# Decoding float64 weights with one shift: bytes landed one off, the sign made by ScalarE

## The chip, the cores and the metric

The kernel runs on one core of one Trainium2 chip. The metric is the device time of one launch in microseconds (us). The kernel before was timed three times: median 725.14 us, lowest 724.97, highest 725.63.

TensorE (PE) multiplies and transposes, VectorE (DVE), ScalarE (ACT) and GpSimd (POOL) do the elementwise work, SyncE (SP) issues the DMAs. Each engine works through its own list of instructions in order.

## The reference

Attention with a window of 128 keys and 4 sink keys, for 4 batches, 8 heads, 768 positions and 64 dimensions a head, and behind it a feed-forward block over the 3072 rows of 512 numbers that the heads make together:

```python
scores = np.where(keep, scale * q @ k.T, -1e9)      # keep: sink or in window
a = np.exp(scores - max); a = a / (sum + 1e-9)
x = (a @ v) -> [3072, 512]
h = x @ w_in                                         # [512, 2048]
g = np.where(h >= 1, h, np.where(h <= -1, 0, (h + 1) ** 2 / 4))
out = g @ w_out                                      # [2048, 512]
```

The weights `w_in` and `w_out` are float64 and are handed to the kernel as 8-byte words; q, k and v are float32.

## The kernel before, in words

**Units and chunks.** A unit is one head of one batch at one half of the positions: three tiles of 128 queries. Eight units (the heads) make a chunk of 384 rows, and there are eight chunks. The attention of chunk c+1 runs beside the feed-forward block of chunk c, so at the start there is only attention, and beside it the decoding of weights.

**One unit** goes through `scores` (three products into PSUM; DVE finds the row maxima while it evacuates, line 253; ACT takes the exponential, line 257; POOL and DVE make the reciprocals of the sums, lines 262 and 263; then three instructions scale the three tiles, lines 273 to 277), `transp` (two groups of TensorE transposes, copied out by ACT, lines 329 and 333) and, for the first 16 units ("native"), `av2`, which multiplies two units at once with their values (line 369; ACT copies the result, line 371, and `split` makes its coarse part, line 475). `NORM` says for a native unit which engine scales which tile: `"vaa"` is DVE for the first and ACT for the other two.

**Weights.** They come as 32 blocks of 128 x 512 float64: 16 of `w_in` and 16 of `w_out` in turn. `weights(n)` fetches block n and up to three after it into raw tiles (512 KB each) and calls `decode`: from the two 32-bit halves of each float64, three DVE instructions (lines 157 to 159) make the bits of a float32; ACT rounds it to the matrix type (line 160) and DVE subtracts to get the remainder (line 161). So a block costs four DVE instructions and one of ACT. `WFIRST = 13` blocks are spread over the attention of the first chunk, the other 19 over the feed-forward block of the first chunk.

**Feed-forward block.** `stage1` makes h for 128 of the 2048 columns and g from it (lines 452 to 455), split into gh and gl (line 456: on POOL in the first chunk, by `GL_POOL`, on DVE in the others); `stage2` multiplies with `w_o`.

**What sets the order.** TensorE's order is that of the program, as `spread` mixes the lists of steps. For the other engines a planner orders the instructions at build time; `issue_after` keeps a decode behind the row maximum issued last. The DMAs of the start stay in program order on SP (`keep_in_program_order`): the values of a pair (`v_s`, two buffers) wait for the product of the pair two before, and the weight blocks behind them in SP's list wait too.

**Rounds.** Between 13 and 54 us TensorE goes through the same round four times: scores of a unit, transposes of the unit before, scores of the next unit, transposes of the first, values product of a finished pair (`av2`). The rounds below are numbered 1 to 4; round 1 takes the scores of units 2 and 3, round 4 those of 8 and 9. From 54 us on the feed-forward block runs beside the attention.

## Time and profile before

| | |
|---|---|
| median of three runs | 725.14 us |
| profiled execution | 726.5 us |
| its span, first to last instruction | 724.8 us |
| mean granted TensorE clock | 0.992 of 2.4 GHz |
| PE, DVE, ACT, POOL busy | 699.7, 529.4, 504.4, 305.7 us |

The profiled execution took 726.5 us, 1.7 us more than its span and 1.4 us more than the median of the timed runs. "Busy" is the time in which an engine has an instruction in work; instructions of DVE and ACT overlap the next one by about 0.1 us, so that a queue that never waits advances by the distance of the starts, not by the durations.

### The profile page before, as it was taken

What the parts mean: (1) busy time and instruction counts of PE and PEld (TensorE: products, weight loads), DVE (VectorE), ACT (ScalarE), POOL (GpSimd) and SP (SyncE); (2) the same over time, 40 slices, a digit from 0 to 9 for tenths busy, and PEclk for the clock granted to TensorE, in tenths of its full rate; (3) what the DMA queues carried; (4) which work ended last, traced back from release to release, by engine and by line L of the source; (5) the groups of instructions that cost most, each with busy time, mean ns of one, the idle gap of its engine ahead of it and who ended that gap; (6) DMA issues with size and microseconds to landing.
All of it is one profiled execution on the core that took longest, in us unless ns stands there. A gap on an engine that the chain in (4) does not pass through costs nothing.

```text
span 724.8 us, 12264 instructions
## 1 busy us (share of the span) xinstructions
PE 699.7 (97%) x3841; PEld 615.6 (85%) x3841; DVE 529.4 (73%) x1393; ACT 504.4 (70%) x1313; POOL 305.7 (42%) x529
## 2 busy tenths in 40 slices
PE   6879999999999999999999999999999999999996
PEld 4547778899989999999889998999989989989895
DVE  8988989578786777687887887878877787833221
ACT  5887677687776777687677877778777867644432
POOL 3002224755453545455564666645556365500000
PEclk9989999999999999999999999999999999999999
DMA  7453453222221322153242533334323342101001
GB/s 291 146 225 127 188 193 121 58 89 58 57 57 33 96 65 66 46 186 114 88 125 64 170 126 115 115 103 137 122 82 127 107 125 74 67 1 44 0 1 48
DMA packets 38568, 73.54 MB, mean 101 GB/s; under 512 B 6752, under 2 KB 21088, under 8 KB 38496
## 3 DMA queue, kind: packets, MB, share of 16 engines
q1 hardware_dynamic: 38496, 72.68, 31.2%
q8 instruction: 32, 0.52, 0.3%
q14 instruction: 40, 0.33, 0.1%
HBM read 66.37 MB, written 6.29 MB: 100 GB/s over the span
## 4 chain that ended last, share of the span: by engine, by line
PE 70%; DVE 13%; ACT 6%; DMA 5%; POOL 3%; issue 2%; POOLq 0%; ACTq 0%; SPq 0%; DVEq 0%
PE h_ps L445 28%; PE o_ps L464 28%; PE ps_a L249 6%; PE ps_a L404 4%; ACT p L257 2%; PE ps_a L336 2%; DVE k_s L233 2%; DMA k_r<-qk 1%; DVE p L277 1%; PE ps_a L369 1%; PE ps_a L326 1%; DMA r<-vx 1%; DVE gl L456 1%; ACT k_s L231 1%; DMA r<-qk 1%
## 5 line engine op out<-in xcount | busy, mean ns | idle before, releaser
L445 PE MATMUL h_ps<-x,wi 128*128 128x384 f32 x1536 | 310.1, 340 | 0.0
L445 PEld LDWEIGHTS h_ps<-x,wi 128*128 128x128 f32 x1536 | 262.7, 188 | 10.8 <-issue 2.7
L464 PE MATMUL o_ps<-w,gh 128*128 128x512 f32 x768 | 243.6, 398 | 0.0
L464 PE MATMUL o_ps<-w,gl 128*128 128x512 f32 x384 | 150.9, 393 | 0.3 <-POOL gl L456 0.3
L464 PEld LDWEIGHTS o_ps<-w,gh 128*128 128x128 f32 x768 | 134.1, 188 | 15.8 <-issue 1.4
L454 DVE SCALAR_TENSOR_TENSOR g<-g,h_ps 128x384 f32<-128x384 f32 x128 | 70.2, 548 | 66.4 <-ACT g L453 65.5
L452 ACT ACTIVATE g<-h_ps,half 128x384 f32<-128x384 f32 x128 | 73.9, 577 | 62.0 <-PE h_ps L445 61.6
L257 ACT ACTIVATE p<-p,peak 128x260 f32<-128x260 f32 (+1 forms) x192 | 94.0, 490 | 30.7 <-DVE peak L253 29.2
L235 POOL TENSOR_TENSOR q_l<-r,q_h 128x384 fp32r<-128x384 f32 x48 | 50.4, 1049 | 131.9 <-ACT q_h L234 121.6
L455 ACT CAST gh<-g 128x384 fp32r<-128x384 f32 x128 | 65.5, 511 | 53.0 <-DVE g L454 52.1
L456 DVE TENSOR_TENSOR gl<-g,gh 128x384 fp32r<-128x384 f32 x112 | 70.2, 627 | 24.7 <-ACT gh L455 23.7
L464 PEld LDWEIGHTS o_ps<-w,gl 128*128 128x128 f32 x384 | 72.0, 188 | 18.2 <-POOL gl L456 0.8
L253 DVE CUSTOM_DVE_ANT_0 p<-ps_a,m 128x260 f32<-128x260 f32 (+1 forms) x176 | 68.2, 398 | 16.6 <-PE ps_a L249 15.9
L233 DVE TENSOR_TENSOR k_s<-k_r,k_s 64x524 fp32r<-64x524 f32 (+1 forms) x44 | 47.2, 1073 | 42.8 <-ACT k_s L231 42.7
L453 ACT ACTIVATE g<-g 128x384 f32<-128x384 f32 x128 | 67.0, 524 | 2.6
L348 POOL TENSOR_SCALAR_AFFINE_SELECT pt<-pt 128x384 fp32r<-128x384 f32 (+1 forms) x96 | 50.3, 525 | 23.8 <-DVE pt L341 21.8
L277 DVE TENSOR_SCALAR p<-p,stat 128x132 f32<-128x132 f32 (+1 forms) x160 | 56.8, 404 | 0.2
L262 POOL TENSOR_SCALAR stat<-stat 128x3 f32<-128x3 f32 x64 | 28.6, 447 | 66.1 <-ACT p L257 61.4
L346 POOL TENSOR_SCALAR_AFFINE_SELECT pt<-pt 128x384 fp32r<-128x384 f32 (+1 forms) x96 | 52.6, 549 | 6.9 <-ACT pt L340 2.7
L404 PEld LDWEIGHTS ps_a<-pt,v_s 128*128 128x128 f32 x304 | 46.5, 188 | 2.2
L404 PE MATMUL ps_a<-pt,v_s 128*128 128x256 f32 (+1 forms) x304 | 46.4, 272 | 0.0
L249 PE MATMUL ps_a<-k_s,q_h 128*128 128x260 f32 (+1 forms) x144 | 40.4, 281 | 4.4 <-DVE sk L343 3.1
(116 smaller groups left out, 986.1 us busy)
## 6 DMA issues: line engine op xcount, KB each, us to landing
r<-qk SPq DMA_DIRECT2D x48, 192.0 KB
k_r<-qk SPq DMA_DIRECT2D x32, 262.0 KB
w<-w_in SPq DMA_DIRECT2D x16, 512.0 KB
w<-w_out SPq DMA_DIRECT2D x16, 512.0 KB
again<-w_in SPq DMA_DIRECT2D x16, 512.0 KB
again<-w_out SPq DMA_DIRECT2D x16, 512.0 KB
out<-o SPq DMA_DIRECT2D x23, 256.0 KB
r<-vx SPq DMA_DIRECT2D x32, 128.0 KB
```

Source lines behind the costliest of these rows:

```text
L249: nc.tensor.matmul(ps[:, lo:260], lhsT=q[:, i * P:(i + 1) * P], rhs=k_s[:, c0:c0 + 260 - lo], start=(j == 0), stop=(j == len(qs) - 1))
L253: found = nc.vector.tensor_tensor_reduce(out=p[:, i, lo:260], in0=ps[:, lo:260], in1=m, scale=-0.125, scalar=3.0e38, op0=ALU.add, op1=ALU. ...
L257: nc.scalar.activation(p[:, i, lo:260], p[:, i, lo:260], AF.Exp, bias=peak_i, scale=-1.0, accum_out=stat[:, i:i + 1])
L277: (nc.gpsimd if eng == "p" else nc.vector).tensor_scalar(p[:, i, lo:260], p[:, i, lo:260], r, None, op0=ALU.mult)
L404: nc.tensor.matmul(z, lhsT=w, rhs=y, start=(n == 0), stop=(n == len(mms) - 1))
L445: nc.tensor.matmul(h_ps[:, :T], lhsT=w_i[j][:, w, ct * P:(ct + 1) * P], rhs=x[:, y, ct], start=(ct == 0 and n == 0), stop=(ct == NCT - 1 a ...
L452: nc.scalar.activation(g, h_ps[:, :T], AF.Relu, bias=half, scale=0.5)
L453: nc.scalar.activation(g, g, AF.Square)
L454: nc.vector.scalar_tensor_tensor(g, g, 1.0, h_ps[:, :T], op0=ALU.min, op1=ALU.max)
L455: nc.scalar.copy(gh, g)
L456: (nc.gpsimd if row0 == GL_POOL else nc.vector).tensor_tensor(gl, g, gh.bitcast(F32), op=ALU.subtract)
L464: nc.tensor.matmul(o_ps[tt], lhsT=gg[:, tt * P:(tt + 1) * P], rhs=w_o[j][:, w], start=(j == 0 and n == 0), stop=(j == NJ - 1 and n == 2))
```

## The change

Four edits go together.

- A raw tile is 8 bytes a partition longer, and the block lands one byte further, from byte 1. The 32-bit word 1 of the tile then holds bytes 3 to 6 of the first float64, so that one shift right by 5 gives the lower 27 bits of the float32. The top byte (sign and upper exponent bits) lies at byte 8, the first of word 2.
- `quick` replaces `decode` for the planned blocks: ACT reads the top bytes as uint8, scales and adds so that the low bits of the float32 which it writes hold the wanted five bits (Relu with a scale and a per-partition bias, into word 2); DVE shifts word 1 in place; one DVE instruction shifts word 2 left by 27 and joins both; then rounding and subtraction as before (`parts`). A block now costs three DVE instructions and two of ACT.
- `NORM` is "vva": DVE scales two tiles of a native unit, ACT one. `GL_POOL` is gone: gl is always made by DVE.
- `WFIRST` is 10: ten blocks beside the first chunk's attention, 22 beside its feed-forward block.

```diff
-GL_POOL = 0
-NORM = "vaa"
+NORM = ("vva", "vva")
-WFIRST = 13
+WFIRST = 10
+STEP = 1.125 + 2.0 ** -12
+BASE = 2.0 ** 23 - 31.5
...
+    base = const.tile([P, 1], F32, name="base")
+    nc.gpsimd.memset(base, BASE)
...
+    def parts(t, w):
+        nc.scalar.copy(t[:, 0], w)
+        nc.vector.tensor_tensor(t[:, 1], w, t[:, 0].bitcast(F32), op=ALU.subtract)
...
+    def quick(t, w, words):
+        x, top = words[:, 1:-1:2], words[:, 2::2]
+        nc.scalar.activation(top.bitcast(F32), words.bitcast(U8)[:, 8::8], AF.Relu, bias=base, scale=STEP)
+        nc.vector.tensor_scalar(x, x, 5, None, op0=ALU.logical_shift_right)
+        nc.vector.scalar_tensor_tensor(w, top, 27, x, op0=ALU.logical_shift_left, op1=ALU.bitwise_or)
+        parts(t, w.bitcast(F32))
...
-                    raw[k] = wpool.tile([P, 2 * DM], I32, name="w")
-                    fetch(raw[k], (w_in, w_out)[k % 2][k // 2].bitcast(I32))
+                    raw[k] = wpool.tile([P, 2 * DM + 2], I32, name="w")
+                    fetch(raw[k].bitcast(U8)[:, 1:8 * DM + 1], (w_in, w_out)[k % 2][k // 2].bitcast(U8))
...
-                decode((w_i, w_o)[i][j], moe.tile([P, DM], I32, name="o"), words)
+                quick((w_i, w_o)[i][j], moe.tile([P, DM], I32, name="o"), raw[n])
...
-            eng = NORM[i] if units.index(u) < NATIVE else "v"
+            eng = NORM[units.index(u) // H][i] if units.index(u) < NATIVE else "v"
...
-        (nc.gpsimd if row0 == GL_POOL else nc.vector).tensor_tensor(gl, g, gh.bitcast(F32), op=ALU.subtract)
+        nc.vector.tensor_tensor(gl, g, gh.bitcast(F32), op=ALU.subtract)
```

The planner puts the lists of DVE and ACT in a new order. On ACT, round 2, from behind the copy of the values product to the scaling of unit 4 (line 275; p_366 is unit 4, p_407 unit 5), before:

```order
L160 CAST wi2_153<-o_358 128x512
L160 CAST w_318<-o_319 128x512
L475 CAST x_657<-xn_169 128x384
L257 ACTIVATE p_366,stat_367<-p_366,peak_97 128x128
L257 ACTIVATE p_366,stat_367<-p_366,peak_97 128x260
L329 COPY pt_335<-ps_a_394 128x2x128
L333 COPY spn3_146<-ps_a_394 4x128
L329 COPY pt_335<-ps_a_400 128x3x128
L257 ACTIVATE p_366,stat_367<-p_366,peak_97 128x260
L257 ACTIVATE p_407,stat_408<-p_407,peak_97 128x128
L257 ACTIVATE p_407,stat_408<-p_407,peak_97 128x260
L275 ACTIVATE p_366<-p_366,stat_367 128x260 x2
```

and now, where line 175 is the new Relu, 273 the exponential and 291 the scaling (w_349 is the first block that is fetched in this round, p_360 unit 4, p_400 unit 5):

```order
L159 CAST w_351<-o_352 128x512
L491 CAST x_634<-xn_171 128x384 [waits Activation_49]
L273 ACTIVATE p_360,stat_361<-p_360,peak_99 128x128 [waits DVE_49,Pool_49]
L273 ACTIVATE p_360,stat_361<-p_360,peak_99 128x260 [waits DVE_49]
L345 COPY pt_328<-ps_a_379 128x2x128 [waits PE_49]
L349 COPY spn3_148<-ps_a_379 4x128
L273 ACTIVATE p_360,stat_361<-p_360,peak_99 128x260 [waits DVE_49]
L175 ACTIVATE w_349<-w_349,base_86 128x512 [waits DMAHW6_49]
L345 COPY pt_328<-ps_a_393 128x3x128 [waits PE_49]
L159 CAST wi2_155<-o_387 128x512 [waits DVE_49]
L273 ACTIVATE p_400,stat_401<-p_400,peak_99 128x128 [waits DVE_49,Pool_49]
L291 ACTIVATE p_360<-p_360,stat_361 128x260 [waits DVE_49,Activation_49]
```

One of the two scalings has left ACT, and a Relu that waits for a DMA has come ahead of the one that is left. In round 4 it is the same (p_544 is unit 8, p_584 unit 9), here from the first exponential to the scaling:

```order
L273 ACTIVATE p_544,stat_545<-p_544,peak_99 128x128 [waits DVE_49,Pool_49]
L345 COPY pt_512<-ps_a_571 128x2x128 [waits PE_49]
L273 ACTIVATE p_544,stat_545<-p_544,peak_99 128x260 [waits DVE_49]
L349 COPY spn3_148<-ps_a_571 4x128
L345 COPY pt_512<-ps_a_577 128x3x128 [waits PE_49]
L175 ACTIVATE w_518<-w_518,base_86 128x512 [waits DMAHW6_49]
L273 ACTIVATE p_544,stat_545<-p_544,peak_99 128x260 [waits DVE_49]
L159 CAST wi4_157<-o_556 128x512 [waits DVE_49]
L273 ACTIVATE p_584,stat_585<-p_584,peak_99 128x128 [waits DVE_49,Pool_49]
L273 ACTIVATE p_584,stat_585<-p_584,peak_99 128x260 [waits DVE_49] x2
L291 ACTIVATE p_544<-p_544,stat_545 128x260 [waits DVE_49,Activation_49]
```

What moved there: the Relu of w_518, which the round's own first fetch brings, stands ahead of the scaling of p_544, and so do all three exponentials of unit 9. On SP, from the block ahead of those values, w_349 stands right behind the values v_s_306:

```order
L149 DMA w_298<-w_out 128x4096 [waits DMAHW4_49]
L149 DMA v_s_306<-vp 128x512 [waits DMAHW5_49,PE_49]
L149 DMA w_349<-w_in 128x4096 [waits DMAHW6_49]
L149 DMA qp_358<-qp 128x776 [waits DMAHW7_49]
L149 DMA w_385<-w_out 128x4096 [waits DMAHW0_49]
L149 DMA v_s_398<-vp 128x512 [waits DMAHW1_49,PE_49]
```

So it cannot be issued before the values product that ends the round before, as was so of the block behind v_s_304 in the kernel before; two blocks a round follow now, where it was three.

## Rows read from the trace of the kernel before

**Rows 1.** The page's second part: the span in 40 slices of 18.1 us, busy tenths of TensorE and its granted clock.
```profile
PE   6879999999999999999999999999999999999996
PEclk9989999999999999999999999999999999999999
```

**Rows 2.** Busy time by stretch: start and end, length, then busy us of PE, PEld, DVE, ACT and POOL with their counts, granted clock, DMA share, GB/s. The second to the fifth row are rounds 1 to 4.
```profile
4.67:12.96 8.29, 6.99 (x19) 4.29 (x19) 7.52 (x36) 4.42 (x17) 1.63 (x6) 1.00 1.00 381
12.96:23.34 10.38, 10.38 (x41) 6.61 (x40) 9.92 (x32) 9.06 (x28) 1.01 (x3) 1.00 0.35 138
23.34:33.53 10.19, 7.92 (x42) 4.96 (x40) 10.05 (x31) 9.24 (x28) 0.46 (x2) 0.83 0.62 222
33.53:43.75 10.22, 7.91 (x42) 4.99 (x40) 9.42 (x29) 8.79 (x27) 0.71 (x2) 0.83 0.61 218
43.75:54.00 10.25, 7.86 (x43) 5.00 (x41) 8.53 (x27) 8.84 (x28) 0.46 (x2) 0.83 0.60 218
...
91.68:112.89 21.21, 21.21 (x110) 15.91 (x109) 19.55 (x42) 15.59 (x42) 6.99 (x7) 1.00 0.50 180
```

**Rows 3.** TensorE in order of time: the transposes of the first unit in rounds 2, 3 and 4, with TensorE's idle time before them and what ended it.
```profile
29.36 0.81 PE L326 MATMUL ps_a<-ident,p 128*128 128x128 f32 x2 [1.38 <-ACT p L275]
...
39.58 0.80 PE L326 MATMUL ps_a<-ident,p 128*128 128x128 f32 x2 [1.86 <-ACT p L275]
...
49.82 0.80 PE L326 MATMUL ps_a<-ident,p 128*128 128x128 f32 x2 [2.05 <-ACT p L275]
```

**Rows 4.** ACT in order of time, round 2, from the copy of the values product to the end of the scaling: start, duration. The distance to the next start is what an instruction costs in a queue that does not wait.
```profile
23.49 0.48 ACT L371 COPY xn<-ps_a 128x384 f32<-128x384 f32 x1 [0.44 <-PE ps_a L369]
23.93 0.62 ACT L160 CAST wi<-o 128x512 fp32r<-128x512 f32 x1
...
24.98 0.51 ACT L475 CAST x<-xn 128x384 fp32r<-128x384 f32 x1
25.39 0.40 ACT L257 ACTIVATE p<-p,peak 128x128 f32<-128x128 f32 x1
...
25.79 0.49 ACT L257 ACTIVATE p<-p,peak 128x260 f32<-128x260 f32 x1
...
26.28 0.35 ACT L329 COPY pt<-ps_a 128x256 f32<-128x256 f32 x1
26.54 0.25 ACT L333 COPY spn<-ps_a 4x128 f32<-4x128 f32 x1
26.69 0.46 ACT L329 COPY pt<-ps_a 128x384 f32<-128x384 f32 x1
27.06 0.51 ACT L257 ACTIVATE p<-p,peak 128x260 f32<-128x260 f32 x1
...
28.81 0.90 ACT L275 ACTIVATE p<-p,stat 128x260 f32<-128x260 f32 x2
29.61 0.60 ACT L160 CAST w<-o 128x512 fp32r<-128x512 f32 x1
```

**Rows 5.** The same in rounds 3 and 4: the copy of the values product, and the instruction that follows the two scalings.
```profile
33.68 0.48 ACT L371 COPY xn<-ps_a 128x384 f32<-128x384 f32 x1 [0.60 <-PE ps_a L369]
...
39.83 0.50 ACT L257 ACTIVATE p<-p,peak 128x260 f32<-128x260 f32 x1
...
43.87 0.48 ACT L371 COPY xn<-ps_a 128x384 f32<-128x384 f32 x1
...
50.08 0.50 ACT L257 ACTIVATE p<-p,peak 128x260 f32<-128x260 f32 x1
```

**Rows 6.** ACT at the start and in round 1: the first scaling of all (unit 0), the scaling of unit 2 and the instruction behind it.
```profile
10.75 0.90 ACT L275 ACTIVATE p<-p,stat 128x260 f32<-128x260 f32 x2
...
18.56 0.90 ACT L275 ACTIVATE p<-p,stat 128x260 f32<-128x260 f32 x2
19.36 0.60 ACT L160 CAST wi<-o 128x512 fp32r<-128x512 f32 x1
```

**Rows 7.** Groups of instructions by line and shape: busy us and mean ns of one, idle time before them. Line 193 is a later step that reads the top byte of every 8 on ACT.
```profile
L193 ACT COPY top<-again 128x512 uint8<-128x512 uint8 x32 | 21.0, 658 | 13.6 <-DMA again<-w_out 8.4 <-DMA again<-w_in 4.9
...
L157 DVE TENSOR_SCALAR o<-w 128x512 int32<-128x512 int32 x32 | 14.8, 463 | 2.3 <-DMA w<-w_in 2.3
...
L160 ACT CAST wi<-o 128x512 fp32r<-128x512 f32 x16 | 9.8, 614 | 1.0 <-DVE o L159 0.7
```

**Rows 8.** SP's issues at the start of round 2 in order of time, and a piece of the chain of waits at 93 us: the issue of a block behind values, and the time to its landing.
```profile
23.48 0.33 SPq L146 DMA_DIRECT2D v_s<-vp  x1
23.86 0.43 SPq L146 DMA_DIRECT2D w<-w_in  x1
...
93.67 3.73 DMA w<-w_in
```

**Rows 9.** POOL and DVE in order of time at 64 us: gl on POOL, and the DVE instruction of line 158 that runs beside it; then line 158 between 9 and 54 us: count, ns of one (least, median, most), first and last start.
```profile
64.48 1.02 POOL L456 TENSOR_TENSOR gl<-g,gh 128x384 fp32r<-128x384 f32 x1 [1.13 <-ACT gh L455]
...
64.68 1.36 DVE L158 SCALAR_TENSOR_TENSOR o<-w,o 128x512 int32<-128x512 int32 x1
...
L158 DVE SCALAR_TENSOR_TENSOR o<-w,o x13: 679/684/689, 11.3 to 50.2; 128x512 int32<-128x512 int32 x13
```

**Rows 10.** What TensorE waited for after 54 us, from the table of waits: us in total, times, longest.
```profile
PE o_ps L464 <- POOL gl L456: 0.3, 1, 0.3
PE ps_a L249 <- POOL q_l L235: 0.3, 1, 0.3
```

More of the change, by code (lines that the diff above doesn't have):

```diff
@@ L159, in decode @@
         nc.vector.scalar_tensor_tensor(w, low, 29, w, op0=ALU.logical_shift_right, op1=ALU.bitwise_or)
-        nc.scalar.copy(t[:, 0], w.bitcast(F32))
-        nc.vector.tensor_tensor(t[:, 1], w.bitcast(F32), t[:, 0].bitcast(F32), op=ALU.subtract)
+        parts(t, w.bitcast(F32))
[4 more added lines that the diff above has]
+        nc.vector.scalar_tensor_tensor(w, top, 27, x, op0=ALU.logical_shift_left, op1=ALU.bitwise_or)
+        parts(t, w.bitcast(F32))
     top = {}
@@ L170, in f @@
                 if k not in raw:
-                    raw[k] = wpool.tile([P, 2 * DM], I32, name="w")
-                    fetch(raw[k], (w_in, w_out)[k % 2][k // 2].bitcast(I32))
-            words = raw[n].rearrange("p (c two) -> p c two", two=2)
+                    raw[k] = wpool.tile([P, 2 * DM + 2], I32, name="w")
+                    fetch(raw[k].bitcast(U8)[:, 1:8 * DM + 1], (w_in, w_out)[k % 2][k // 2].bitcast(U8))
             if i:
-                w_o[j] = wpool.tile([P, 2, DM], F32R, name="w")
+                w_o[j] = wpool.tile([P, 2 * DM + 2], F32R, name="w")[:, :2 * DM].rearrange("p (h c) -> p h c", h=2)
             with tc.issue_after(last_max[-1].ins) if last_max else nullcontext():
-                decode((w_i, w_o)[i][j], moe.tile([P, DM], I32, name="o"), words)
+                quick((w_i, w_o)[i][j], moe.tile([P, DM], I32, name="o"), raw[n])
         return f
```

## The prediction

> **What bounds the kernel now.** I read the page first, then the busy time by stretch, then the order in time of the stretch that is not full. The slices show TensorE at 9 tenths or more everywhere but in the first three [rows 1], so only the first 54 us, and the dense stretch behind them if it should break, can change the time. By stretch, TensorE is busy 21.21 of 21.21 us in a dense piece, but only 7.9 of 10.2 us in each of rounds 2 to 4; round 1 is full, 10.38 of 10.38 [rows 2]. There TensorE ran at the lower of its two levels: transposes after an idle time of 1.4 to 2.1 us take the same slow form [rows 3], and the granted clock of rounds 2 to 4 is 0.83 on the mean [rows 2].
>
> At first sight DVE bounds the rounds: 10.05 of 10.19 us busy in round 2. But in round 4 it is busy 8.53 and in round 3 9.42, and these take 10.25 and 10.22 us, no less [rows 2]. One and a half us less of DVE have bought nothing in the kernel before itself. What each round waits for is written in the three rows of TensorE: the transposes of the first unit of the round stand 1.38, 1.86 and 2.05 us until ACT has scaled that unit [rows 3]. So a round is a chain through ACT's queue: copy of the values product, casts, exponentials, copies of transposes, scaling. From the start of the first to the end of the scaling it takes 6.12 us in round 2 (23.49 to 29.61) [rows 4], 6.15 in round 3 (33.68 to 39.83) and 6.21 in round 4 (43.87 to 50.08) [rows 5]. The other 4 us, transposes and the values product at the low clock, follow on it. I therefore price the change by what stands in ACT's queue ahead of that scaling, and take the rest of the round as it is.
>
> **The price list of ACT.** By distances of starts [rows 4]: copy of the product 0.39 (its row shows 0.44 with a wait, duration 0.48 less the overlap of 0.1), cast of a weight 0.51, of x 0.41, exponential of 128 columns 0.40, of 260 columns 0.49, the three copies of transposes 0.26, 0.15 and 0.37, a scaling 0.40 (0.80 for two). The new Relu is not in this trace. Its nearest row is the ACT copy that also reads one byte of every eight, 658 ns against 614 for a weight cast [rows 7]: 0.56 by distance. Bounds: not under the cast's 0.51, since it has as many elements, and not over 0.66, the whole duration.
>
> **The parts.**
>
> *DVE.* A block loses a two-input instruction (0.68 us by line 158 [rows 9], 0.6 by distance), and the shift that stays is like line 157, 0.46 [rows 7]; in place and strided on both sides it costs between that and 0.68. With ten blocks of three instructions for thirteen of four, 30 for 52, DVE loses some 10 to 12 us of its 38 in rounds 1 to 4 [rows 2], and gets back one scaling a unit, eight times at most the 0.45 that ACT takes for it [rows 4]. I count the gain at nothing, since round 4 shows that DVE's time is covered by ACT's chain; the rival below takes it at its worth.
>
> *Round 1* runs from ACT's first scaling at 10.75 to the scaling of unit 2, which ended at 19.36 [rows 6]. In the new order ACT has up to there: six Relus, three casts, three scalings instead of six, five exponentials, the copies of two units: 6 x 0.56 + 3 x 0.51 + 3 x 0.40 + (3 x 0.49 + 2 x 0.40) + 2 x 0.78 = 9.9 us, so 20.6. The scaling is 1.3 us later. TensorE, dense until then, stands for it and has 1.0 us of transposes before the values product; some of the delay was its own queue, so I take +0.9 (bounds 0 and 1.3). The DMAs of these six blocks are early enough: they are issued one behind the other at the start.
>
> *Rounds 2 to 4: the wait for a block.* In each round ACT's first Relu takes the block that SP issues right behind the values, and those go only when the values product of the round before is done. In round 2 that block was issued at 23.86, 0.37 us after the copy began [rows 8]. In the same place at 93 us a block needed 3.73 us from issue to landing [rows 8]. So it is there 4.1 us after the copy. For the lower bound I take 3.4 (about 0.79 MB, values and block, at the 381 GB/s of the start [rows 2], and 1.0 us of start-up). When does ACT reach the Relu? Round 2: 0.39 + 0.51 + 0.41 + 0.40 + 0.49 + 0.26 + 0.15 + 0.49 = 3.1; it waits 1.0. Behind it stand Relu 0.56, copy 0.37, cast 0.51, exponential 0.40 and the scaling 0.40: the end is at 4.1 + 2.24 = 6.3, against 6.12: **+0.2**. Round 3 reaches it at 3.5; behind it 0.56 + 0.40 + 0.51 + 0.49 + 0.40, end at 6.45 against 6.15: **+0.3**. Round 4 reaches it at 3.0; behind it 0.56, 0.49 + 0.51 + 0.40 + 2 x 0.49 and the scaling 0.40: 7.4 against 6.21: **+1.2**. With the lower bound of the landing these three become -0.5, -0.3 and +0.5. Everything behind a waiting Relu waits with it: exponentials, copies that free PSUM for the next scores, and so TensorE.
>
> A row on landing one byte off does not exist. A block's 512 KB take 1.4 us at 381 GB/s [rows 2]; I take the same here. The Trainium skill, "DMA: Bandwidth & Descriptors", section "How a descriptor splits into AXI transactions", speaks against it: a piece that does not start on a 256-byte boundary costs one transaction more, its first one mostly empty. If that holds for a row of 4096 bytes written one byte off, it is 17 for 16, an estimate of 0.1 us a block and +0.3 us on the whole sum. No run here shows it yet.
>
> *From 54 us on.* TensorE is full there while ACT is busy 15.6 and DVE 19.6 of 21.2 us [rows 2]. Per such piece ACT gets some seven Relus (3.9 us) and loses two scalings (0.8): 18.7 of 21.2, still not full. DVE loses 0.6 for each of seven blocks and gets gl, 0.6 each. That costs it nothing: while POOL made gl, the DVE instruction beside it took 1.36 us instead of 0.68 [rows 9]. TensorE's waits for POOL, 0.3 for gl and 0.3 for q_l [rows 10], should go: **-0.6** (bounds 0, and -0.6). A broken dense stretch would cost up to 1 us; I take 0.
>
> **Sum.** 0.9 + 0.2 + 0.3 + 1.2 - 0.6 = +2.0 us. The profiled execution would go from 726.5 to 728.5 (span 726.8); the median lies 1.4 us under the profiled time, so 725.14 becomes **727.1**. With the bounds: from -0.9 (0 - 0.5 - 0.3 + 0.5 - 0.6) to +4 (1.3, 1.7 and 1.0), 724.2 to 729.1.
>
> **The rivals.**
>
> *DVE was the bound after all (faster).* For it: round 2 is full of DVE, and ACT's row there shows a wait for DVE's maximum hidden in its 6.12 us; without it and the wait for the product the list sums to 5.7. Then ACT's queue, freed of one scaling a unit and with fewer casts, sets the pace. A round of ACT is 8.8 us busy [rows 2], less two scalings (0.8), 1.2 casts (0.6), plus two Relus (1.1): 8.5; at the share of 0.91 that ACT reached in round 2 (9.24 of 10.19) a round takes 9.35, 0.9 less: -2.6 for three, nothing for round 1, where TensorE itself is full, and -0.3 for the waits on POOL: 722.2. It decides if the blocks land within 3 us of the copy, or if ACT reaches its Relus late. Against it: round 4.
>
> *Nothing moves.* Landing at 3.4 and half of the price in round 1 cancel: +0.1, 725.2. For it: TensorE's order and work are the same, and the low clock makes up half of a late start of the values product.
>
> *The odd byte makes the DMAs slow (slower by much).* If a block takes twice 1.4 us, each round's Relu starts 1.4 later, 3 x 1.4 = 4.2, and in round 1 the sixth block lands some 8 us later where ACT has 3 us to spare, +5: about 736. Point from which it decides: a block of over 2 us. For it speaks no row, against it only that a row of the block is one long piece.
>
> **How the numbers follow.** Forecast 0.42, the rival with DVE 0.28, nothing 0.18, slow DMAs and a broken dense stretch together 0.12. 0.2% is 1.45 us and about what a measurement of this kernel can tell from no change. Of the forecast a fifth lies within it (small waits), so slower 0.33 + 0.12 = 0.45, same 0.18 + 0.09 = 0.27, faster 0.28. The likeliest case's own range is 725.5 to 729.1. The range for 8 in 10 takes in the rival with DVE and a little over the upper bound: 721.8 to 730.0; left out are the slow DMAs and the far end of the faster rival.
>
> **What would show it.** Right: in rounds 2 to 4 ACT idle before the first Relu (line 175) with the DMA of w as releaser, 0.5 to 1 us each; TensorE's transposes in round 4 waiting over 2.5 us for ACT's scaling (line 291); DVE clearly under 8 us a round; first product of the feed-forward block at 56 to 57 us instead of 54.4. Wrong: that product before 53; a Relu of 0.4 us or less; no idle before it. TensorE idle in the dense stretch would speak for a broken stretch; landings of over 5 us behind an issue, for slow DMAs.

## The result, and the profile after

The changed kernel took 734.65 us (median of 4, 732.35 to 736.05) against 725.12 us (724.97 to 725.63) for the kernel before: a ratio of 1.0127, 95% interval 1.0100 to 1.0154. It is slower by 9.5 us; 2 were forecast. The execution with a profile took 734.9 us (span 733.1). Run once more beside the last experiments it came to 1.0126 (1.0108 to 1.0143).

The page after, its head and two lines of the slices, beside [rows 1]:

```profile
span 733.1 us, 12240 instructions
PE 704.5 (96%) x3841; PEld 617.4 (84%) x3841; DVE 517.4 (71%) x1393; ACT 517.3 (71%) x1329; POOL 284.8 (39%) x514
PE   6869999899999999999999999999989999999996
PEclk9989999999999999999999999999999999999999
```

DVE is busy 12 us less and ACT 13 us more. TensorE has new gaps, in the third slice, in the eighth (128 to 147 us) and in the thirtieth; the last costs nothing in sum (below). Where the time went is read from the busy time by stretch: the same rounds 1 to 4 as in [rows 2] (round 1 counted from the same 12.96, though its first scores start at 13.23 now), then three pieces of the dense stretch. Columns: stretch, length, then for PE, PEld, DVE, ACT, POOL the busy time and instructions; granted clock of TensorE, DMA share, GB/s.

```profile
12.96:25.50 12.54, 11.99 (x43) 6.96 (x41) 8.56 (x28) 10.71 (x32) 0.46 (x2) 1.00 0.27 106
25.50:36.05 10.55, 8.17 (x42) 4.94 (x40) 7.19 (x25) 8.62 (x26) 0.49 (x2) 0.87 0.44 164
36.05:46.36 10.31, 7.98 (x43) 4.96 (x41) 6.84 (x25) 8.60 (x26) 0.45 (x2) 0.83 0.45 166
46.36:57.82 11.46, 7.69 (x42) 5.15 (x41) 7.13 (x25) 8.73 (x26) 0.56 (x2) 0.83 0.43 149
64.00:74.00 10.00, 9.32 (x47) 6.97 (x47) 8.37 (x24) 9.99 (x28) 0.66 (x2) 1.00 0.23 93
104.00:114.00 10.00, 10.00 (x48) 7.30 (x47) 8.36 (x26) 10.00 (x27) 0.68 (x1) 1.00 0.66 223
117.00:140.00 23.00, 20.16 (x117) 16.80 (x116) 20.54 (x51) 18.16 (x47) 8.57 (x12) 0.93 0.38 118
```

DVE is down to 7 us a round, and no round is shorter for it. In the dense stretch ACT is now full where blocks are decoded (9.99 and 10.00 of 10), and from 117 to 140 us TensorE misses 2.8 us. The line of the Relu, TensorE's longest wait in the rounds (at the transposes of round 4), and its waits from 60 to 160 us (what was waited for, us in total, times, longest):

```profile
L175 ACT ACTIVATE w<-w,base x32: 737/760/797, 10.8 to 132.1; 128x512 f32<-128x512 uint8 x32
```

```profile
54.15 0.69 PE L342 MATMUL ps_a<-ident,p 128*128 128x128 f32 x2 [3.21 <-DVE p L293]
```

```profile
PE ps_a L265 <- POOL k_s L249: 1.9, 1, 1.9
PE ps_a L265 <- POOL q_l L251: 0.9, 1, 0.9
PE h_ps L461 <- DVE g L470: 0.7, 1, 0.7
```

Two marks cut the span into three: the first product of the feed-forward block, and SP's issue of the first output tile of the second row of tokens. Before they stand at 54.4 and 234.5 us, after at 58.2 and 243.1. So the stretch ahead of the first product lost 3.8 us, the next one 4.8 (184.9 for 180.1), and the rest nothing (490.0 for 490.3). The waits listed above account for 3.5 of the 4.8.

### The profile page after: what moved, and what is told of

Same layout as the page of the kernel before. It is cut to its first block, busy times and chain, and to the rows that moved or that the text cites. A ratio compares the mean times of both kernels' runs of the same rounds, so it can differ in the third digit from the quotient of the medians.

```text
span 733.1 us, 12240 instructions
## 1 busy us (share of the span) xinstructions
PE 704.5 (96%) x3841; PEld 617.4 (84%) x3841; DVE 517.4 (71%) x1393; ACT 517.3 (71%) x1329; POOL 284.8 (39%) x514
## 4 chain that ended last, share of the span: by engine, by line
PE 69%; DVE 11%; ACT 10%; DMA 6%; issue 2%; POOL 2%; SPq 0%; ACTq 0%; POOLq 0%; DVEq 0%
PE o_ps L480 28%; PE h_ps L461 28%; PE ps_a L265 4%; PE ps_a L420 4%; ACT p L273 3%; PE ps_a L385 2%; PE ps_a L352 2%; DVE p L293 2%; DMA w<-w_in 1%; DVE k_s L249 1%; ACT w L175 1%; DMA w<-w_out 1%; DVE gl L472 1%; DMA out<-o 1%; DVE p L285 1%
## 5 line engine op out<-in xcount | busy, mean ns | idle before, releaser
L472 DVE TENSOR_TENSOR gl<-g,gh 128x384 fp32r<-128x384 f32 x128 | 78.9, 616 | 28.0 <-ACT gh L471 27.0
L293 DVE TENSOR_SCALAR p<-p,stat 128x132 f32<-128x132 f32 (+2 forms) x176 | 60.5, 396 | 0.7
```

The lines of the kernel that those rows point to most:

```text
L293: (nc.gpsimd if eng == "p" else nc.vector).tensor_scalar(p[:, i, lo:260], p[:, i, lo:260], r, None, op0=ALU.mult)
L472: nc.vector.tensor_tensor(gl, g, gh.bitcast(F32), op=ALU.subtract)
```

## The experiments

All runs in one table. Ratios are to the kernel before on the same chip (725.1 to 727.3 us); the other columns come from each run's one profiled execution: the first product, and from there to the mark in the second row. Behind that mark these executions take 487.2 to 492.8 us (490.3 before), a scatter that was not followed up, so the two columns do not add up to the ratio. e5_no_top, e6_odd_byte, e11_aligned and e19_no_top_fill leave out or misread a part of the decode, so that their weights are others. In rows of runs that add lines, a line's number is up to five higher.

| run | what | ratio (95%) | first product | to second row |
|---|---|---|---|---|
| | kernel before | 1 | 54.4 | 180.1 |
| | changed kernel | 1.0127 (1.0100-1.0154) | 58.2 | 184.9 |
| e20_after_again | the same again | 1.0126 (1.0108-1.0143) | 58.1 | 185.8 |
| e1_decode_only | new decode, old settings | 1.0097 (1.0058-1.0135) | 61.8 | 179.2 |
| e2_tuning_only | old decode, new settings | 1.0185 (1.0156-1.0214) | 54.4 | 193.5 |
| e18_10first | before, ten blocks first | 1.0110 (1.0090-1.0131) | 53.7 | 188.5 |
| e7_13first | after, thirteen first | 1.0075 (1.0051-1.0100) | 57.8 | 180.8 |
| e9_gl_pool | after, gl on POOL | 1.0087 (1.0065-1.0110) | 59.1 | 182.3 |
| e5_no_top | after, no Relu | 1.0020 (1.0000-1.0039) | 52.3 | 182.1 |
| e3_top_pool | after, Relu's step on POOL | 1.0082 (1.0052-1.0113) | 58.9 | 182.8 |
| e4_ahead6 | after, six fetched ahead | 1.0140 (1.0087-1.0194) | 59.7 | 182.2 |
| e10_pool_13_6 | these two, thirteen first | 1.0174 (1.0144-1.0203) | 59.0 | 184.2 |
| e6_odd_byte | before, one byte further | 1.0031 (1.0009-1.0053) | 56.5 | 181.6 |
| e11_aligned | after, not one byte further | 1.0091 (1.0065-1.0117) | 59.6 | 183.2 |
| e12_fill_after | after, 4 needless products | 1.0034 (1.0008-1.0059) | 54.4 | 184.0 |
| e14_fill_before | before, 4 needless products | 1.0000 (0.9984-1.0017) | 54.8 | 180.3 |
| e16_before_fill8 | before, 8 of them | 1.0016 (0.9995-1.0038) | 53.4 | 180.6 |
| e15_13_fill8 | after, 13 first, 8 of them | 1.0071 (1.0050-1.0091) | 55.8 | 181.5 |
| e17_13_gl_fill8 | the same, gl on POOL | 1.0095 (1.0062-1.0127) | 57.4 | 180.5 |
| e19_no_top_fill | no Relu, 13 first, 4 of them | 0.9921 (0.9899-0.9943) | 49.0 | 183.1 |

**The two halves of the change.** The first theory was the prediction's: the Relus in ACT's queue. The first rival put it down to the three settings.

```diff
-NORM = ("vva", "vva")
+GL_POOL = 0
+NORM = ("vaa", "vaa")
...
-WFIRST = 10
+WFIRST = 13
...
-        nc.vector.tensor_tensor(gl, g, gh.bitcast(F32), op=ALU.subtract)
+        (nc.gpsimd if row0 == GL_POOL else nc.vector).tensor_tensor(gl, g, gh.bitcast(F32), op=ALU.subtract)
```

> The changed kernel with the three settings put back: 13 blocks first, one scaling of three on VectorE for every unit of the first sixteen, the difference gl of the first row of tokens on GpSimd. What is left of the change is the landing one byte further and the new decode. Theory 1 (the Relus in ScalarE's queue cost it: 0.66 us each and a wait for the block's DMA, ahead of the scalings in the rounds and ahead of the casts of k and q behind 115 us): the time stays well above the kernel before, 733 to 742 us; three more Relus stand before the first product of the feed-forward block, which comes at 59 to 62 us, while the stretch from 60 to 160 us has fewer Relus and stands still less than the 4 us of the changed kernel. Rival A (the settings cost it): 724 to 727 us, and the first product at 54 to 55 us.

The edit of the other half, on the kernel before:

```diff
-GL_POOL = 0
-NORM = "vaa"
+GL_POOL = -1
+NORM = "vva"
...
-WFIRST = 13
+WFIRST = 10
```

> The kernel before with the three settings of the change alone: ten blocks first, two scalings of three on VectorE in the first sixteen units, gl always on VectorE; old landing, old decode. Theory 1 (the Relus cost it): 722 to 727 us, about the kernel before, since the rounds hang on ScalarE and lose one scaling and one or two casts of it, while VectorE gets one scaling more. Rival A (the settings cost it): 731 us or more, with the first product of the feed-forward block at 57 us or later or a break of the dense stretch at 115 to 130 us.

Beside the kernel before both halves cost, in different places. The decode alone delays the first product by 7.4 us and leaves the dense stretch whole (179.2). The settings alone leave the first product where it was and lose 13.4 us behind it, which theory 1 had not expected. The halves do not add up: with the old settings the new decode is the slower one (1.0097 against 1), with the new settings the faster one (1.0127 against 1.0185), since it takes back 8.6 of the 13.4 us behind the first product (184.9 against 193.5) and loses 3.8 ahead of it. TensorE's waits from 60 to 165 us in the run with the settings alone:

```profile
PE ps_a L249 <- POOL k_s L233: 7.7, 2, 6.3
PE ps_a L249 <- POOL q_l L235: 2.0, 2, 1.1
PE ps_a L326 <- DVE peak L253: 0.3, 1, 0.3
```

**Which setting.** One at a time: `WFIRST = 10` for 13 in the kernel before; the reverse in the changed kernel; gl of the first row back on POOL in the changed kernel. `NORM` alone was not run.

> The kernel before with one setting alone: ten blocks before the first product instead of thirteen; old landing, old decode, old scalings, gl on GpSimd. If ten blocks first is what breaks the stretch behind the first product (VectorE gets three more blocks of four instructions there, some 8 us, in a stretch where it was busy 9 to 10 of 10 us): first product at 52 to 54 us, a stop of 3 us or more near 115 to 130 us, 727 to 733 us. If it takes gl on VectorE as well: no stop of over 1 us, 723 to 726 us.

> The changed kernel with thirteen blocks before the first product instead of ten, all else as changed. If the stop near 129 us comes from the three blocks that the change put behind the first product: the stretch from 115 to 160 us is full again (44 of 45 us or more), the first product moves to 60 to 62 us, and the time is 731 to 735 us. If the stop comes from gl on VectorE: it stays, at 2.5 us or more, with the first product at 60 to 62 us, 736 us or more.

> The changed kernel with the difference gl of the first row of tokens on GpSimd again, all else as changed. If gl on VectorE broke the stretch behind 115 us (sixteen instructions of 0.6 us there): no stop there, 730 to 732 us, the first product still at 58 us. If the Relus alone broke it: the stop stays at 2.5 us or more, 734 to 736 us.

Ten blocks first alone costs the old decode 8.4 us behind the first product (188.5), and thirteen first repairs 4.1 of the changed kernel's 4.8 (180.8). With gl on POOL 2.6 come back as well, as it too unloads DVE there (8.41 of 10 us busy from 114 to 124 us, 9.13 in the changed kernel), but this run's first product was later (59.1). What `NORM` does shows only in pairs of profiles: with the new decode and thirteen first the product comes at 61.8 with "vaa" and at 57.8 with "vva", and gl, the other difference of the two, is made only behind it. The three forecasts were met in kind and missed in size: 734.1 us for 727 to 733 with ten first alone, a first product at 57.8 for 60 to 62 with thirteen, and 733.3 us, between the two numbers named, with gl on POOL.

The way in which ten blocks first cost time is SP's queue, where a block's DMA waits until a raw tile is free and the loads of the next unit stand behind it. Issues of the second loads of k behind 60 us, in the kernel before, the changed kernel, the one with ten first alone and the one with thirteen first:

```profile
115.15 0.36 SPq L146 DMA_DIRECT2D k_r<-qk  x1
```

```profile
123.15 0.36 SPq L149 DMA_DIRECT2D k_r<-qk  x1
```

```profile
121.49 0.33 SPq L146 DMA_DIRECT2D k_r<-qk  x1
```

```profile
116.90 0.33 SPq L149 DMA_DIRECT2D k_r<-qk  x1
```

So the load of k that is late by 8 us after is late by 6.3 with ten first alone and by 1.8 with thirteen. Counted from each run's own first product it is later by 4.2, by 7.0, and with thirteen first earlier by 1.6; what the stretch lost is 4.8, 8.4 and 0.7. What frees the tiles is DVE's decode. In the run with ten first alone SP stands 7.05 us ahead of the block that it issues at 120.67, and the load of k follows directly behind it. These are SP's longest waits for DVE from 54 to 140 us in that run, and the busy time where TensorE stops; DVE is full (9.90 of 10, where the kernel before has 9.59, with TensorE at 9.71):

```profile
SPq L146 <- DVE peak L253: 13.9, 4, 7.0
SPq L146 <- DVE o L159: 13.7, 3, 6.6
```

```profile
114.00:124.00 10.00, 8.49 (x48) 7.43 (x47) 9.90 (x21) 7.27 (x21) 3.10 (x4) 1.00 0.41 121
124.00:134.00 10.00, 6.33 (x29) 5.56 (x28) 8.11 (x19) 4.44 (x13) 3.71 (x4) 0.83 0.32 114
```

In the changed kernel the same place has one more link. ACT stood 1.60 us with a Relu whose block had just been fetched, and the casts of k and q came behind it (ACT's timeline, start and duration):

```profile
126.26 0.79 ACT L175 ACTIVATE w<-w,base 128x512 f32<-128x512 uint8 x1 [1.60 <-DMA w<-w_in]
...
127.86 0.51 ACT L247 CAST k_s<-k_r 128x392 fp32r<-128x392 f32 x1
128.28 0.51 ACT L471 CAST gh<-g 128x384 fp32r<-128x384 f32 x1
128.69 0.51 ACT L250 CAST q_h<-r 128x384 fp32r<-128x384 f32 x1
```

**The Relu.** Left out, moved to POOL, and given blocks that are there in time:

```diff
-        nc.scalar.activation(top.bitcast(F32), words.bitcast(U8)[:, 8::8], AF.Relu, bias=base, scale=STEP)
...
-        nc.vector.scalar_tensor_tensor(w, top, 27, x, op0=ALU.logical_shift_left, op1=ALU.bitwise_or)
+        nc.vector.scalar_tensor_tensor(w, x, 0x38000000, x, op0=ALU.bitwise_or, op1=ALU.bitwise_or)
```

> The changed kernel without the Relu: the step that makes sign and top exponent bits is left out, and the join puts a constant in the place of the upper exponent bits, so every weight comes out positive. VectorE's work on a block, the landing and the settings stay as changed. Theory 1 (the Relus cost it all): the time falls by 9 us or more, to 721 to 726 us, the first product comes at 52 to 54.5 us, and there is no stop at 129 us. Theory 1 with VectorE as a second bound: under 721 us. Rival A (the settings) and rival B (a byte further makes the DMAs slow): it stays at 731 us or more.

```diff
-        nc.scalar.activation(top.bitcast(F32), words.bitcast(U8)[:, 8::8], AF.Relu, bias=base, scale=STEP)
+        nc.gpsimd.tensor_scalar(top.bitcast(F32), words.bitcast(U8)[:, 8::8], STEP, BASE, op0=ALU.mult, op1=ALU.add)
```

> The changed kernel with the step that makes sign and top exponent bits on GpSimd (a multiply and an add) in place of ScalarE's Relu; GpSimd was busy 7.0 of the first 60 us and 3.1 of the next 55. Theory 1 (what costs is the place of the step in ScalarE's queue): the first product comes back to 52 to 55 us and the stretch behind it does not stand still, 722 to 728 us, provided that GpSimd's step takes under 1.5 us. Rival A (the settings cost it whatever the Relu does): 732 us or more. Rival C (GpSimd holds VectorE up at the port that they share, as the difference on GpSimd did before the change): VectorE's shift and join become longer by a third or more and the time stays at 730 us or above.

```diff
-AHEAD = 3
+AHEAD = 6
```

> The changed kernel with blocks fetched up to six ahead instead of three, so that a Relu finds its block landed. TensorE's order is the same. Theory 1 with the DMA as its larger part (it is the waiting Relu that holds ScalarE): the first product at 55 to 56.5 us instead of 58.2, no Relu idle for its DMA, 728 to 731 us. Theory 1 with the Relu's own time as its larger part: 732 to 736 us, the idle before the Relu is gone and the rounds hardly shorter.

Without the Relu the first product comes at 52.3, 5.9 us earlier than after: the decode's part of the loss, and more (727.2 us, where theory 1 had asked for 726 at most). On POOL TensorE hardly waits in the dense stretch (0.5 us in all from 60 to 160), though it still takes 182.8 up to the second row, and the first product stays late, against theory 1. POOL's timeline in round 3 shows why: its step waits for the block, and the small sum from which the scalings come stands behind it, though ACT's last exponential of that unit had ended at 39.7:

```profile
40.31 0.65 POOL L175 TENSOR_SCALAR w<-w 128x512 f32<-128x512 uint8 x1 [7.70 <-DMA w<-w_in]
41.04 0.28 POOL L278 TENSOR_SCALAR stat<-stat 128x3 f32<-128x3 f32 x1
```

The 732.4 us of this run are what the rival with the settings had asked for (732 or more), but the run gives this other reason for them. The third rival, that POOL holds DVE up, is not borne out: DVE's shift and join took 423 and 685 ns at the median, 424 and 689 in the changed kernel.

With blocks fetched six ahead ACT's Relus wait 0.9 us for them before 60 us instead of 1.7, and the first product is no earlier (59.7). So that wait was halved, not removed, and halving it brought nothing: it is not mainly the wait for the DMA that holds the rounds.

**The odd byte.** The kernel before with the blocks one byte further (its three instructions then read shifted words), and the changed kernel without it:

```diff
...
-                    fetch(raw[k], (w_in, w_out)[k % 2][k // 2].bitcast(I32))
+                    fetch(raw[k].bitcast(U8)[:, 1:8 * DM + 1], (w_in, w_out)[k % 2][k // 2].bitcast(U8))
...
```

> The kernel before with the blocks landing one byte further, and its three instructions of VectorE on a block kept in number, but reading the shifted words (the sign is left out and the upper exponent bits are a constant). Old settings. Theory 1: 724.5 to 727 us, a block lands within 3.9 us of its issue where it is fetched alone. Rival B (the odd byte costs the DMAs): 729 us or more, with landings over 5 us and VectorE's first instruction on a block waiting for the DMA.

```diff
-        nc.scalar.activation(top.bitcast(F32), words.bitcast(U8)[:, 8::8], AF.Relu, bias=base, scale=STEP)
+        nc.scalar.activation(top.bitcast(F32), words.bitcast(U8)[:, 7:8 * DM:8], AF.Relu, bias=base, scale=STEP)
...
-                    fetch(raw[k].bitcast(U8)[:, 1:8 * DM + 1], (w_in, w_out)[k % 2][k // 2].bitcast(U8))
+                    fetch(raw[k].bitcast(U8)[:, :8 * DM], (w_in, w_out)[k % 2][k // 2].bitcast(U8))
```

> The changed kernel with the blocks landing where they did before (no byte further), every instruction kept; the decode then reads the wrong bits, so the weights are others. Rival B (the odd byte costs the DMAs): 730 us or less. All other theories: 732 to 737 us, as the changed kernel, the same landing times.

The first run's 729.35 us lie just inside the rival's number (729 or more), the second's 733.16 outside (730 or less). But the rival's cause is not there. A block that is fetched alone lands as fast as before: from the chain of waits of the changed kernel, then of the kernel with ten blocks first (old landing), against 3.73 in [rows 8]:

```profile
116.12 3.42 DMA w<-w_out
122.71 3.52 DMA w<-w_in
```

```profile
120.67 3.68 DMA w<-w_in
...
130.16 3.50 DMA w<-w_out
```

And the packets of 4096 bytes in which the blocks come took 159 ns at the median in the kernel before, in the run with the odd byte and in the changed kernel alike. Yet both ratios lean the same way, by some 0.3%. In the run with the odd byte ACT's list and the times of DVE's decode are those of the kernel before up to the first product; the difference there is TensorE's clock (0.50 from 30 to 36 and from 36 to 42 us, against 0.73 and 0.84). In the other run the planner ordered the lists of ACT and DVE anew, so that its small difference can't be put down to the byte. The DMAs are not slower; whether 1 or 2 us hang on the byte in another way stays open.

**TensorE's clock.** In the runs so far the rounds 2 to 4 took from 8.3 to 12.2 us, the short ones at a granted clock of 1.00. In the run without the Relu, two rounds that follow each other:

```profile
23.81:32.09 8.28, 6.23 (x41) 4.40 (x42) 6.80 (x25) 7.40 (x24) 0.81 (x2) 1.00 0.61 209
32.09:41.94 9.85, 7.69 (x41) 4.81 (x42) 6.89 (x25) 7.55 (x24) 0.69 (x2) 0.83 0.49 173
```

DVE and ACT have the same work in both. What differs is what TensorE does behind its wait. In round 2 of the kernel before, after 1.38 us of idle [rows 3], everything runs in the long form, 4.17 us from 29.36 to the next scores at 33.53; in the run without the Relu the same instructions, after 1.82 us of idle, took 2.32 (29.64 to 31.96). The values products of both:

```profile
30.96 2.40 PE L369 MATMUL ps_a<-pt,v_s 128*64 128x128 f32 x12
33.15 0.46 PE L369 MATMUL ps_a<-spn,v_s 128*64 128x128 f32 x4
```

```profile
29.64 0.50 PE L341 MATMUL ps_a<-ident,p 128*128 128x128 f32 x2 [1.82 <-DVE p L292]
...
30.51 1.30 PE L384 MATMUL ps_a<-pt,v_s 128*64 128x128 f32 x12
31.64 0.39 PE L384 MATMUL ps_a<-spn,v_s 128*64 128x128 f32 x4
```

The first kernel is at the lower of the two levels (1.2 GHz), the second the upper (2.4). From this came theory 2: a round loses some 1.9 us to the clock, not to a queue. To test it TensorE got needless work into its wait, in both kernels, first 4 products (`FILL`), then 8.

```diff
+FILL = 4
...
+            if not part and units.index(u) in (4, 6, 8):
+                busy = ps_h.tile([P, 512], F32, name="h_ps")
+                for _ in range(FILL):
+                    nc.tensor.matmul(busy[:, :T], lhsT=w_i[0][:, 0, :P], rhs=w_i[0][:, 0, :T], start=True, stop=True)
             for i in range(i0, CT):
```

> The changed kernel with four needless products of 128x384 on TensorE in each of the rounds 2 to 4, put where it waits for the scaling (their result is used by nothing). Theory 2 (the wait lets TensorE's clock fall, and the low clock is what makes a round long): the granted clock of the rounds goes from 0.83 to over 0.95, the transposes and products behind the wait run in the short form, a round takes 8.5 to 9.5 us instead of 10.3 to 11.5, first product at 54 to 56 us, 729 to 732 us. Theory 1 alone (ScalarE's queue): the rounds stay over 10 us, 734 to 736 us. If the fill is in the way: longer than the changed kernel.

> The kernel before with the same four needless products on TensorE in each of the rounds 2 to 4. Theory 2: rounds of 8.2 to 9 us instead of 10.2 and a clock of over 0.95 in them, first product at 50 to 52 us instead of 54.4, 721 to 723 us: faster than both kernels. Theory 1 alone: 725 us, rounds of 10.2 us.

> The changed kernel with three things at once: the step for sign and top exponent bits on GpSimd, thirteen blocks first, and blocks fetched up to six ahead. In the run with GpSimd alone its step waited for the block's DMA in GpSimd's queue, ahead of the small sum on which the scalings hang (1.4 us in round 3); with blocks fetched earlier that wait should go. Theory 1 in a wider form (what costs is a step that stands, or waits, in a queue ahead of the scalings; what broke the stretch behind 115 us is ten blocks first): first product at 53 to 56 us, no stop behind 60 us, 721 to 727 us. Theory 2 (the rounds' length is set by TensorE's clock, which falls after its wait in each round, and not by the queue): rounds of 10 to 12 us at a granted clock of 0.85 or less, first product 57 us or later, 727 to 731 us.

> The changed kernel with thirteen blocks first and eight needless products of TensorE (2 us by the 0.97 us of four) in each of the rounds 2 to 4. If the two causes found are all of it (the clock that falls behind TensorE's wait in the rounds, and three more blocks behind the first product): rounds of 8.5 to 9.5 us at a clock of over 0.95, first product at 53 to 55 us, no stop of more than 1 us behind it, 721 to 726 us. If the longer queue of ScalarE counts by itself: 727 us or more though the clock is high.

> The kernel before with eight needless products in each of the rounds 2 to 4 in place of the four of the run before, which left waits of 0.75, 2.46 and 1.30 us behind them and a clock of 0.87 and 0.84 in two rounds. Theory 2: no wait of over 1 us, a clock of over 0.95 in all three rounds, rounds of 8.3 to 9.5 us, 720 to 724 us. Rival: the rounds of the kernel before hang on ScalarE and VectorE, not on the clock; 725 to 728 us.

> As the run with thirteen blocks first and eight needless products, and the difference gl of the first row of tokens on GpSimd again. If VectorE's queue still broke the stretch behind the first product there: 1 to 2 us less than that run, with VectorE under 9.5 of 10 us everywhere from 64 to 134 us. If not: within 1 us of it, or slower by the time for which GpSimd holds VectorE up.

Four products bring the changed kernel from 1.0127 to 1.0034, as theory 2 asked; the kernel before they leave where it was, against it, and with eight as well (1.0016, 726.8 us, in the range of theory 2's rival). The rounds tell more. First the changed kernel with four, then the same with thirteen blocks first and eight, then the kernel before with eight:

```profile
25.16:33.99 8.83, 7.19 (x45) 4.47 (x46) 6.63 (x23) 8.10 (x25) 0.49 (x2) 1.00 0.53 196
33.99:43.05 9.06, 7.46 (x45) 4.68 (x46) 7.39 (x27) 8.88 (x28) 0.45 (x2) 1.00 0.50 189
43.05:53.81 10.76, 8.90 (x45) 5.66 (x45) 6.79 (x25) 8.47 (x27) 0.45 (x2) 0.75 0.45 159
```

```profile
35.69:44.61 8.92, 7.80 (x49) 5.25 (x50) 8.23 (x27) 8.92 (x28) 0.79 (x2) 1.00 0.65 250
44.61:55.51 10.90, 9.34 (x49) 6.58 (x50) 8.70 (x30) 10.90 (x32) 0.46 (x2) 0.84 0.55 205
```

```profile
23.70:32.58 8.88, 8.17 (x49) 5.74 (x50) 8.24 (x28) 8.20 (x26) 0.80 (x2) 1.00 0.70 254
32.58:44.21 11.63, 9.18 (x49) 5.92 (x49) 10.91 (x33) 9.74 (x30) 0.54 (x2) 0.88 0.54 192
```

In the changed kernel rounds 2 and 3 are 3.0 us shorter than without the products, at a clock of 1.00; round 4, at 0.75, is 0.7 shorter. The edit is not quite clean: the planner, which knows of the products, ordered the lists of ACT and DVE anew. In rounds 2 and 3 the same instructions of ACT stand ahead of the scaling as after; in round 4 one exponential fewer does, so that round shows nothing about the clock. And of the 7.6 us between the two profiled executions 2.8 lie behind the second row, in the scatter named above.

Where the clock is kept another limit shows. In the kernel before the busy time points to DVE: what one round saves the next has to decode (10.91 of 11.63 us). In the changed kernel with thirteen blocks it points to ACT, busy 8.92 of 8.92 and 10.90 of 10.90 us; there eight products bring the first product forward by 2.0 us and the ratio not at all (1.0071 for 1.0075). So needless products won time in one kernel of three, the changed one with ten blocks; with thirteen theory 1 holds, as the run without the Relu below shows. Three more forecasts missed: thirteen first with eight products (1.0071 where 721 to 726 us was asked), the same with gl on POOL (1.0095; a round of 11.86 us at a clock of 0.71), and POOL with blocks six ahead (1.0174: POOL's step at 0.66 to 1.1 us still stood ahead of the sum, and TensorE waited 3.5 and 4.0 us in rounds 2 and 3).

The last two runs: the changed kernel again, and the upper bound of what the decode could bring, with the Relu left out, thirteen blocks first and four needless products.

> The changed kernel, not altered, on the chip of this call: the scale for the others, since the kernel before took 725.1 to 727.3 us on the chips so far. Every theory: 1.010 to 1.015 of the kernel before.

Its rounds 2 to 4:

```profile
25.59:34.25 8.66, 6.93 (x41) 4.33 (x42) 6.63 (x23) 8.09 (x25) 0.48 (x2) 1.00 0.55 200
34.25:46.12 11.87, 8.61 (x41) 5.08 (x41) 7.34 (x27) 8.99 (x28) 0.51 (x2) 0.75 0.41 144
46.12:57.78 11.66, 7.96 (x41) 5.33 (x42) 7.17 (x25) 8.72 (x26) 0.56 (x2) 0.82 0.39 147
```

The program is the same to the instruction, and round 2 keeps the clock by itself; but round 3 takes 11.87 us, and the first product comes at 58.1 as before (58.2). So a round that kept the clock was paid back in the next one, which theory 2 does not explain. It also shows how far a single profile can be read: in those of e1, e3, e4, e6 and e11 one round ran at 0.50 to 0.52 from end to end, so that their first products carry a part of the clock.

> The changed kernel without the Relu (sign and upper exponent bits left out), with thirteen blocks first and four needless products in each of the rounds 2 to 4: what the decode could be worth if its top step were free. If VectorE's saving has a worth that ScalarE's Relu and the clock hid: first product at 50 to 52 us, no stop behind it, 719 to 723 us. If ScalarE's queue or the low clock binds even so: 724 to 727 us.

```profile
23.56:32.07 8.51, 7.36 (x45) 5.21 (x46) 7.26 (x26) 7.91 (x25) 1.16 (x2) 1.00 0.71 265
32.07:40.21 8.14, 7.08 (x45) 4.59 (x46) 8.02 (x29) 7.55 (x26) 1.02 (x2) 1.00 0.75 274
40.21:48.68 8.47, 7.16 (x45) 4.65 (x45) 8.02 (x29) 8.25 (x26) 0.69 (x2) 1.00 0.74 264
```

Three rounds in 25.1 us: without the Relu, with thirteen blocks first and the products, the changed kernel is 5.7 us faster than the kernel before (0.9921), which the products alone did not speed up. That is what the change could bring if the top bits were free and the clock kept; how much of it is DVE's saving and how much the scaling that left ACT was not taken apart. With the Relu, thirteen blocks and eight products the three rounds take 28.9 (9.03, 8.92 and 10.90); that is ACT's price, with a part for the clock of the third. No version that computes the reference was faster than the kernel before.

## Why the prediction was wrong

**The step that failed most** is the one on the stretch from 54 us on, forecast at -0.6 with "a broken dense stretch would cost up to 1 us; I take 0". It measured +4.8. The sum for ACT there was right: 18.44 us busy of the 21.21 from 95.50 to 116.71, for 18.7 forecast. But the step weighed what ACT and DVE gain and lose per block against their idle time, and did not ask for what the three blocks more that now fall into this stretch stand in front of: SP's queue, where the loads of k and q come behind them. Ten blocks first had been entered as relief of the rounds alone. Thirteen first took 4.1 of the 4.8 away, and ten first in the kernel before cost 8.4.

**Round 1** was forecast at +0.9 with 1.3 as its bound, and measured +2.2 (12.54 for 10.38). The Relu was mis-sized: 0.56 us by distance was taken, 0.65 measured (10.77 to 11.42), with the upper bound of 0.66 named and not taken. Six of them ahead of unit 2's scaling make 0.5 us; that scaling began at 20.89 and so ended 0.7 later than the 20.6 worked out. The cover counted on there, 1.0 us of transposes, did not hold either: TensorE, in its long form and all but full (11.99 of 12.54), came to these transposes at 20.83, already 1.5 us later than before (19.34). So most of the delay stood ahead of the scaling that was counted. In the run without the Relu the next round begins at 23.81 instead of 25.50: most of the 2.2 is the Relus'.

**Rounds 2 to 4** were forecast at +0.2, +0.3 and +1.2, in sum +1.7. By the stretches above they measured +0.4, +0.1 and +1.2; the sum is right. In the second run of the changed kernel they were 8.66, 11.87 and 11.66, the same sum in other parts, so the single terms were luck. The signs came for the most part as named: Relus idle for their DMA (0.89, 0.17 and 0.65 us in rounds 2 to 4), DVE under 8 us, transposes of round 4 idle for 3.21 us (but for DVE's scaling, line 293, not ACT's: two of three are DVE's now). That the Relu waits for its block is real, but with blocks six ahead it was half as long and the rounds took no less (33.3 us for 32.3). So that wait was not the main thing that set the rounds, and the sum owes something to luck as well. The first product came at 58.2, beyond the 56 to 57 named. The 1.0 us of start-up in the lower bound of the landing stands in no row of the prediction; a block with no other block ahead of it had its first packet 0.95 to 1.7 us after the issue in the kernel before.

**DVE's saving at nothing** came true in the rounds, on an argument that was only half of it. In round 4 of the kernel before, with less DVE, the part behind TensorE's wait takes the same long form as in round 2 (transposes of 0.80 and 0.81 us, values products of 2.40). "I take the rest of the round as it is" hid 1.9 us a round, which had a say in whether the saving could show. Behind the first product the saving was not nothing: it is most likely what takes the settings' 193.5 us back to 184.9.

**The rivals.** "DVE was the bound" fell for this change, though its mechanism may stand where clock and Relu are out of the way (e19_no_top_fill). The 736 us of the rival with the odd byte were near by luck: they were worked out from slow DMAs alone, which were not found. The broken dense stretch, which came, shared a chance of 0.12 with them and was priced at up to 1 us. The estimate of 17 transactions for 16, drawn there from the Trainium skill, "DMA: Bandwidth & Descriptors", section "How a descriptor splits into AXI transactions", is not borne out by the landings (3.42 and 3.52 us against 3.50 to 3.73) nor by the packets (159 ns in both). That section speaks of bytes that are read, while here it is the landing that is odd; and by its rule the last of the 17 would be all but empty, not the first, as the prediction had it. "Nothing moves" fell with the interval, which begins at 1.0100.

## What to carry to other kernels

When a setting moves work out of a stretch, price it where it arrives, with what stands behind it in every in-order queue there, the DMA queue first. A saving on a nearly full engine that is paid on another nearly full one has to be summed on both. Where TensorE waits each round, look at the length of what follows the wait: needless products in the wait can show how much of a round is clock, once the order of the other engines is the same in both runs.

## What was not expected of the hardware

- The granted clock shows 1.00 in round 1 while the transposes there have the long form (in the changed kernel 1.08, 0.42 and 0.85 us from 20.83 on, as in its round 4 at 0.83). At the start the durations tell the level, not the column.
- A wait is followed by the long form in some rounds and not in others: in the run without the Relu 1.82 us of idle in round 2 left the short form, 1.48 in round 3 did not. This may be part of why the four runs of the changed kernel lie 3.7 us apart, where those of the kernel before beside them lie within 0.7; that is not shown.
- ACT took 0.76 us for 512 bytes read eight apart and written as float32 eight apart, 0.65 by distance, against 0.51 for a cast of as many elements. POOL's median for the same step, with a multiply and an add, was 0.79.
